# Two layers of linear attention and MLP in split fp32: split weights kept in DRAM, and a set of reorderings

## The chip, the cores and the metric

The kernel runs on one core of one Trainium2 chip. The time is the device time of one execution in microseconds (us), lower is better. A core has a matrix engine (PE, with a queue of its own for weight loads, PEld), a vector engine (DVE), an activation engine (ACT), a third engine for elementwise work (POOL), and SP, which here only issues transfers. Each engine runs its instructions in order. SBUF is the on-chip memory, PSUM the eight banks that PE writes, DRAM the memory outside.

## The reference

Two layers, each an attention block (A) and an MLP block (B) with residuals, on 2048 rows of 576 features, with the same weights in both layers:

```python
def _A_ref(x, wqkv, w_phi, wo):
    q, k, v = ...                                  # 32 heads of 18 features, from x @ wqkv
    pq = jnp.einsum("bhsd,hdf->bhsf", q, w_phi)
    pk = jnp.einsum("bhsd,hdf->bhsf", k, w_phi)
    phi_q = jnp.concatenate([_softmax(pq, axis=-1), _softmax(-pq, axis=-1)], axis=-1)
    phi_k = jnp.concatenate([_softmax(pk, axis=-1), _softmax(-pk, axis=-1)], axis=-1)
    kv = jnp.einsum("bhsf,bhsd->bhfd", phi_k, v)
    z  = jnp.einsum("bhsf->bhf", phi_k)
    num = jnp.einsum("bhqf,bhfd->bhqd", phi_q, kv)
    den = jnp.einsum("bhqf,bhf->bhq", phi_q, z)[..., None] + 1e-6
    return (num / den) @ wo                        # heads joined again

def _B_ref(x, w1, b1, w2, b2):                     # 576 -> 4608 -> 576
    h = relu(x @ w1 + b1) ** 2
    return h @ w2 + b2

for _ in range(2):
    x = x + _A_ref(_layernorm(x), A_wqkv, A_w_phi, A_wo)
    x = x + _B_ref(_layernorm(x), B_w1, B_b1, B_w2, B_b2)
```

kv and z are sums over all 2048 rows: no output of a layer's attention can be made before every row's keys and values are in them.

## The kernel before

*Precision.* Each fp32 matrix is split in a high part (`h`, rounded to the matrix engine's fp32r by a copy on ACT) and a low part (`l`, the rest, by a subtraction on DVE or POOL), and a product of two matrices is three: high x high, low x high, high x low. `piece_tiles` gives the two tiles of one half (288 columns) of a 576x576 weight, 128 partitions x 1440; `wpiece` loads the raw weights into a staging tile (tag "wraw", two buffers) and makes the split; `wpair` does both halves, for v, keys, queries ("q", "k", with w_phi folded in, from the DRAM tensor `wf`) or the output ("o"). The pieces have the tags "whi" and "wlo", two buffers each, so one pair fills them; a few pairs use "s2" and "h1" (TAGS_B) instead.

*Stages.* The rows are four blocks of 512, each of four tiles of 128.
1. `g_fold` multiplies the query and key weights with w_phi, stores them as `wf`, and leaves the split of keys and v in SBUF (`kpair`, `vpair`). The norm of block 0 (`g_norm`) is woven in.
2. Keys and values of the blocks of layer 0 (`g_keys`): `make_v`, `make_raw` (projections, `project`, L435), the softmaxes on DVE, ACT and POOL, then `kv_tile` (L527), which adds one tile's phi_k^T v to the sums.
3. `barrier`: the last keys and the queries of two blocks while the sums are completed, then `sums_operands`, which makes the operands of the next products from the sums (kt, L585, from kq, L580, is its last group of heads), `g_phi`, and `g_out`, the attention's output and norm.
4. `g_mlp` of two blocks (`first`: weights; `hidden`, L820; `square`, L827 to L830; `second`, L838 and L847), each with the attention of other blocks woven in (`back_first`, `back_second`).
5. `g_pair`: the MLP of the last two blocks at once, its first product by the seven-product scheme (`products`, L1128), then its second product for one block with the first and for the other alone (`seconds`, L1147 and L1157). In layer 0 the norms, keys and values of layer 1 for three blocks are woven into `seconds` (`back_keys`).
6. Layer 1 from stage 3.

*Order.* A program lays out each engine's instructions ahead of the run, by their order in the source and by when it expects their inputs. `weave(main, other, rate)` interleaves two generators by the costs that they yield; `tc.issue_after(x)` puts instructions behind instruction x on x's engine; `held(gen, keys)` does so for a whole generator, with x the latest `dense["last"]` (the end of the last `square` on DVE), `dense["squared"]` (its end on ACT) and so on. All transfers of weights, x and hidden values are issued by SP in one order, and a transfer whose buffer is not free holds up those behind it. Work banks of PSUM come from `wtile`: two of tag "w" and the banks in `spare["tags"]`.

The softmax of one tile of keys in stage 2 or 5 ends with POOL's scaling (L495), and `kv_tile` waits for it. In layer 1, `kv_tile` writes a work bank for the first eight tiles, and DVE adds it:

```python
        first = 0 if layer == 0 else (NB - 2) * NT
        if n == first:
            st["ps"] = ps_a.tile([P, TB], F32, tag="acc0", name=f"kvp{layer}")
        ...
        stay, last = n >= first, n == NB * NT - 1
        pt = st["ps"] if stay else wtile(f"{name}k")
```

## Time and profile before

| | |
|---|---|
| median of 3 runs | 2557.3 us (2551.11 to 2559.26) |
| the profiled execution | 2557.62 us, of which 2555.9 us from the first to the last instruction |
| busy, of 2555.9 us | PE 2489.1, DVE 1634.6, ACT 1304.2, POOL 971.8 |
| mean granted clock of PE | 0.991 |
| moved by DMA | 312.99 MB, mean 122 GB/s |
| stages | keys of layer 0 from about 36 us, barriers from 160 and 1410 us, `seconds` of layer 0 from about 1168 to 1388 us |

A row of the waits reads: waiting engine, line and tile, then who released it, total us, times, longest. A row of the timeline reads: start us, length us, engine, line, operation, out<-in, shapes, count, and in brackets the idle time before it with its releaser. A stretch's row gives, for each engine, busy us and number of instructions, then the granted clock of PE, the share of the time that the 16 DMA engines were busy and what they moved.

### The profile page before, as it was taken

How to read it: one execution, taken by the hardware profiler on the slowest of the kernel's cores; microseconds unless marked ns; L12 is line 12 of the kernel's file. 1: busy time of each engine (PE TensorE's matmuls, PEld its weight loads, DVE VectorE, ACT ScalarE, POOL GpSimd, SP SyncE). 2: the span in 40 equal slices, each digit the busy share in tenths (PEclk: the TensorE clock that was granted, in tenths of full speed). 3: DMA queues.
4: the chain of work that ended last, by engine and by line, in shares of the span. 5: the costliest groups of instructions: out<-in, count | busy, mean ns of one | idle time of the engine just before them, and what ended most of it. 6: DMA issues, size and time to landing. Idle time of an engine off the chain costs nothing. (4 is left out here: it accounts for less than half of the span.)

```text
span 2555.9 us, 41504 instructions
## 1 busy us (share of the span) xinstructions
PE 2489.1 (97%) x15108; PEld 2182.6 (85%) x15108; DVE 1634.6 (64%) x2570; ACT 1304.2 (51%) x2293; POOL 971.8 (38%) x1101
## 2 busy tenths in 40 slices
PE   8998999999999999999999989999999999999999
PEld 7998888889888888888889988888888888888888
DVE  7777857555866655555777769484658665555444
ACT  4333555354546666664443435553545466666643
POOL 3544313212335555551434533032123445555322
PEclk9999999999999999999999999999999999999999
DMA  8102432344334433338543133333453344333363
GB/s 252 57 23 72 153 111 83 107 141 165 112 117 126 136 118 98 112 102 265 180 128 115 46 111 110 101 89 107 139 183 90 124 130 144 109 101 104 110 201 128
DMA packets 257224, 312.99 MB, mean 122 GB/s; under 512 B 29818, under 2 KB 175482, under 8 KB 254458
## 3 DMA queue, kind: packets, MB, share of 16 engines
q1 hardware_dynamic: 255760, 307.64, 38.7%
q8 instruction: 118, 1.93, 0.3%
q10 hardware_dynamic: 1258, 2.70, 0.3%
q14 instruction: 88, 0.72, 0.1%
HBM read 255.42 MB, written 54.82 MB: 121 GB/s over the span
## 5 line engine op out<-in xcount | busy, mean ns | idle before, releaser
L1118 POOL TENSOR_TENSOR m_ps<-m_pr,m_ps 128x128 fp32r<-128x128 f32 x144 | 121.9, 847 | 319.2 <-ACT m_ps L1116 264.8
L1117 DVE TENSOR_TENSOR m_ps<-m_pr,m_ps 128x448 fp32r<-128x448 f32 x144 | 93.9, 652 | 153.5 <-ACT m_ps L1116 151.2
L1157 PE MATMUL m_pacc<-m_ps,m_phb 128*128 128x448 f32 x864 | 188.5, 366 | 0.0
L1157 PEld LDWEIGHTS m_pacc<-m_ps,m_phb 128*128 128x128 f32 x864 | 162.2, 188 | 18.0
L1116 ACT ACTIVATE m_ps<-m_pr 128x576 fp32r<-128x576 f32 x144 | 97.9, 680 | 132.3 <-issue 88.5
L1157 PE MATMUL m_pacacc<-m_ps,m_phc 128*128 128x448 f32 x648 | 146.0, 369 | 0.0
L1157 PEld LDWEIGHTS m_pacacc<-m_ps,m_phc 128*128 128x128 f32 x648 | 123.3, 191 | 10.1
L1138 DVE TENSOR_TENSOR m_phb<-m_pz,m_phb 128x512 fp32r<-128x512 f32 x72 | 56.5, 784 | 115.9 <-ACT m_pz L1137 114.4
L820 PE MATMUL m_1ph<-t1onh,m_1h 128*128 128x512 f32 (+1 forms) x380 | 100.7, 390 | 4.5 <-ACT m_1hr L827 2.4
L820 PE MATMUL m_3ph<-t0onh,m_3h 128*128 128x512 f32 (+1 forms) x380 | 98.8, 386 | 2.8 <-ACT m_3hr L827 2.4
L847 PE MATMUL m_2acc<-m_2s,m_2hb 128*128 128x448 f32 x432 | 100.1, 365 | 0.0
L847 PE MATMUL m_0acc<-m_0s,m_0hb 128*128 128x448 f32 x432 | 100.1, 365 | 0.0
L847 PE MATMUL m_3acc<-m_3s,m_3hb 128*128 128x448 f32 x432 | 99.7, 366 | 0.0
L847 PE MATMUL m_1acc<-m_1s,m_1hb 128*128 128x448 f32 x432 | 99.7, 366 | 0.0
L820 PE MATMUL m_0ph<-a_0nh,m_0h 128*128 128x512 f32 (+1 forms) x380 | 97.7, 384 | 0.0
L820 PE MATMUL m_2ph<-a_2nh,m_2h 128*128 128x512 f32 (+1 forms) x380 | 97.7, 384 | 0.0
L847 PEld LDWEIGHTS m_2acc<-m_2s,m_2hb 128*128 128x128 f32 x432 | 81.0, 188 | 10.6 <-ACT m_2hb L828 0.2
L847 PEld LDWEIGHTS m_0acc<-m_0s,m_0hb 128*128 128x128 f32 x432 | 81.0, 188 | 10.7 <-ACT m_0hb L828 0.2
L847 PEld LDWEIGHTS m_3acc<-m_3s,m_3hb 128*128 128x128 f32 x432 | 81.0, 188 | 10.6 <-ACT m_3hb L828 0.2
L847 PEld LDWEIGHTS m_1acc<-m_1s,m_1hb 128*128 128x128 f32 x432 | 81.0, 188 | 10.5
L820 PEld LDWEIGHTS m_1ph<-t1onh,m_1h 128*128 128x128 f32 x380 | 70.2, 193 | 19.2 <-ACT m_1hr L827 3.2
L810 POOL TENSOR_TENSOR m_1s<-m_1r,m_1s 128x128 fp32r<-128x128 f32 x36 | 27.0, 749 | 151.7 <-ACT m_1s L806 134.8
(2504 smaller groups left out, 7464.3 us busy)
## 6 DMA issues: line engine op xcount, KB each, us to landing
m_pr<-in_B_w SPq DMA_DIRECT2D x144, 288.0 KB
m_pr<-in_B_w SPq DMA_DIRECT2D x72, 256.0 KB
hd<-m_pu SPq DMA_DIRECT2D x72, 256.0 KB
m_pg<-hd SPq DMA_DIRECT2D x72, 256.0 KB
m_3r<-in_B_w SPq DMA_DIRECT2D x36, 288.0 KB
m_2r<-in_B_w SPq DMA_DIRECT2D x36, 288.0 KB
m_1r<-in_B_w SPq DMA_DIRECT2D x36, 288.0 KB
m_0r<-in_B_w SPq DMA_DIRECT2D x36, 288.0 KB
```

The costliest lines, as they stand in the source:

```text
L810: nc.gpsimd.tensor_sub(s2[:, D + R : 2 * D], r2[:, R:], s2[:, R:D].bitcast(F32))
L820: nc.tensor.matmul(ph[:, cols], a, m, start=(k == 0), stop=(k == len(ops) - 1))
L847: nc.tensor.matmul(acc[t][:, :R], a[:, rows], m, start=(f == 0 and k == 0), stop=(f == NF - 1 and k == 2))
L1116: nc.scalar.activation(s2[:, :D], r2, AF.Copy)
L1117: nc.vector.tensor_sub(s2[:, D : D + R], r2[:, :R], s2[:, :R].bitcast(F32))
L1118: nc.gpsimd.tensor_sub(s2[:, D + R : 2 * D], r2[:, R:], s2[:, R:D].bitcast(F32))
L1138: nc.vector.tensor_sub(hl, r, hh.bitcast(F32))
L1157: nc.tensor.matmul(accs[b][t][:, :R], a[:, rows], m, start=(g == 0 and k == 0), stop=(g == NF - 1 and k == 2))
```

## The change

1. Split weights in DRAM. `wsplit` holds the high and low parts of v, keys, queries and output. The first two are stored from `vpair` and `kpair` after the fold (`keep_split`); the other two are made in ten steps woven into layer 0's keys (`g_split`). `wpair` then loads the parts into the pieces' tiles, with no staging tile and no split, but for pairs in TAGS_B (the barrier's queries and the last keys of layer 1), which are loaded and split as before.
2. In `g_fold` the norm of block 0 starts three steps later and DVE's part of it is issued behind the latest copy of a fold.
3. `kv_tile` of layer 1 accumulates in the bank acc4 throughout; a block's last tile is issued after the next block's norm, and `spare["tags"]` stays empty in `seconds`.
4. `sums_operands` leaves its last group to a function that `barrier` calls after the other block's queries, its matmuls behind the last projection.
5. `g_features` is held behind "last" and "squared"; the low part of the second weights in the first two steps of an MLP goes behind the norm's last split ("normed").
6. `g_norm` with `fine` takes all four tiles' scaling before the transposes, which become one pipeline; its tile has five buffers.
7. At the end of `g_mlp` the first product of the pair (`then`) comes before the last row sums, and the adds of the last 128 columns come last. At the last product two steps of `back_keys` are taken early.

```diff
+    wsplit = {w: [dram.tile([P, 2 * NC * HP], F32, name=f"ws{w}{p}") for p in "hl"] for w in "qkvo"}
+    def idle(n, gen):
+        yield from (1.0 for _ in range(n))
+        yield from gen
...
-            nc.vector.tensor_copy(wt[:w, : n * P], pt[:w, : n * P])
+            dense["folded"] = nc.vector.tensor_copy(wt[:w, : n * P], pt[:w, : n * P])
...
-    def wpair(which, name, tags=TAGS_A, low=None):
-        if which == "v":
-            return [wpiece(wqkv, 2 * D + h * HP, f"{name}v{h}", tags) for h in range(2)]
+    def wpair(which, name, tags=TAGS_A):
+        if tags is TAGS_B:
+            return [wpiece(wf, (which == "k") * D + h * HP, f"{name}{which}{h}", tags) for h in range(2)]
+        return [wloaded(which, h, f"{name}{which}{h}", tags) for h in range(2)]
+
+    def wloaded(which, half, name, tags):
+        pair = piece_tiles(name, tags)
+        regions = [(slice(0, P), 0, NC)]
         if which == "o":
-            return [wpiece(wo, h * HP, f"{name}o{h}", tags, heads=True, low=low) for h in range(2)]
-        return [wpiece(wf, (which == "k") * D + h * HP, f"{name}{which}{h}", tags) for h in range(2)]
+            regions = [(slice(0, GW), 0, NG - 1), (slice(0, gw[-1]), NG - 1, NG)]
+        for piece, kept in zip(pair, wsplit[which]):
+            for p, c0, c1 in regions:
+                at = half * NC * HP
+                nc.sync.dma_start(piece[p, c0:c1].rearrange("p c n -> p (c n)").bitcast(F32),
+                                  kept[p, at + c0 * HP : at + c1 * HP])
+        return pair
+
+    def keep_split(which, pair):
+        for half in range(2):
+            for piece, kept in zip(pair[half], wsplit[which]):
+                nc.sync.dma_start(kept[:, half * NC * HP : (half + 1) * NC * HP],
+                                  piece.rearrange("p c n -> p (c n)").bitcast(F32))
+
+    def g_split():
+        for c in range(NC):
+            for which in "oq":
+                raw = sb.tile([P, D], F32, tag="r2", name=f"ws{which}r{c}")
+                ...                                   # one load of raw from wo or wf
+                both = cst.tile([P, 2 * NG * GW], F32R, tag="kbh" if which == "o" else "kbl", name=f"ws{which}s{c}")
+                hi, lo = both[:w, :D], both[:w, D : 2 * D]
+                nc.scalar.activation(hi, raw[:w], AF.Copy)
+                yield
+                nc.gpsimd.tensor_sub(lo, raw[:w], hi.bitcast(F32))
+                for part, kept in zip((hi, lo), wsplit[which]):
+                    nc.sync.dma_start(kept[:w].rearrange("p (h c n) -> p h c n", h=2, c=NC)[:, :, c],
+                                      part.rearrange("p (h n) -> p h n", h=2).bitcast(F32))
+                yield
...
-        for half in range(2):
-            for t in range(2):
-                apart(half * 2 + t)
-                yield 2.2
-            yield from pipeline(3, (lambda i: cross(half * 3 + i), lambda i: split(half * 3 + i)), (0.3, 0.6))
+        for t in range(NT):
+            apart(t)
+            yield 2.2
+        yield from pipeline(3 * NT // 2, (cross, split), (0.3, 0.6))
...
-        if n == first:
-            st["ps"] = ps_a.tile([P, TB], F32, tag="acc0", name=f"kvp{layer}")
+        if n == 0:
+            st["ps"] = ps_a.tile([P, TB], F32, tag=f"acc{KC * layer}", name=f"kvp{layer}")
...
-        else:
-            nc.vector.tensor_add(kv, po, kv)
...
+        def last_group():
+            ...                                       # kq as before
+            with tc.issue_after(dense["projected"].ins):
+                for s in range(2):
+                    nc.tensor.matmul(p3[:, s], own[:, s].rearrange("p q f -> p (q f)"),
+                                     place.rearrange("p q d -> p (q d)"), start=True, stop=True)
+            keep(p3, [k[:w, :, last, :w] for k in (kbh, kbl)])
+        return last_group
...
-                                 (2.6, 0.4, 3.0, 2.8, 1.2)))
+                                 (2.6, 0.4, 3.0, 2.8, 1.2)), ("last", "squared"))
...
-        def pieces():
-            with tc.issue_after(behind.ins) if behind else nullcontext():
-                return wpair("o", name, low=nc.gpsimd if parts > 1 else None)
+        pair = wpair("o", name)
...
+            with tc.issue_after(dense["normed"].ins) if behind else nullcontext():
                 nc.vector.tensor_sub(s2[:, D : D + R], r2[:, :R], s2[:, :R].bitcast(F32))
...
+        if then:
+            then()
+        for t in range(NT):
+            ...                                       # the four x tiles are loaded here
         by_rows(NF - 1, range(2), range(3))
...
-        if then:
-            then()
         by_rows(NF - 1, range(2, NT), range(3))
         for t, x in enumerate(after):
             nc.vector.tensor_add(x[:, :R], acc[t][:, :R], x[:, :R])
+        for t, x in enumerate(after):
+            nc.vector.tensor_add(x[:, R:], p3[:, t], x[:, R:])
...
-        sums_operands(layer)
+        last_group = sums_operands(layer)
...
         drain(queries)
+        last_group()
...
-    weave(g_fold(kpair, vpair), g_norm(load_x(0), xT[0], "n0_0"), 0.5)
+    weave(g_fold(kpair, vpair), idle(3, held(g_norm(load_x(0), xT[0], "n0_0"), ("folded",))), 0.5)
+    keep_split("v", vpair)
+    keep_split("k", kpair)
+    splits = g_split()
...                                                   # g_keys: next(splits, None) twice a tile
-                stages = (raw, start, lambda t: soft_exp(es[t]), end, lambda t: None)
-                if not last:
-                    stages += (lambda t: kv_tile(1, vts[t], es[t], f"kv{m}_{t}"),)
+                def keep_sums(t):
+                    if not last:
+                        late.append((vts[t], es[t], f"kv{m}_{t}"))
+                        if len(late) > 1:
+                            kv_tile(1, *late.pop(0))
...
-        drain(products)
-        spare["tags"] = ["acc4"]
-        weave(seconds, iter(()) if layer else back_keys(), 4.0)
+        back = iter(()) if layer else back_keys()
+        for k, _ in enumerate(products):
+            if k == NP - 1:
+                next(back, None)
+                next(back, None)
+        weave(seconds, back, 4.0)
```

## The prediction

> **What bounds the kernel now.** I read the page first, then the waits of the matrix engine (PE), then stretches around its longest waits, and last the queue that issues the loads.

> ```profile
> span 2555.9 us, 41504 instructions
> PE 2489.1 (97%) x15108; PEld 2182.6 (85%) x15108; DVE 1634.6 (64%) x2570; ACT 1304.2 (51%) x2293; POOL 971.8 (38%) x1101
> ...
> PEclk9999999999999999999999999999999999999999
> ```

> PE is busy for 2489.1 of 2555.9 us, so all that an edit can win is in the other 66.8 us and in matmuls that ran slowly. The change neither adds nor drops a matmul that counts (one zeroing matmul moves). DVE at 64% and ACT at 51% have room on average: taking work from them is worth only what PE waits for. That list is the waits of PE (who waited for whom, us in total, times, longest):

> ```profile
> PE kt L585 <- DVE kq L580: 7.4, 2, 4.4
> PE kv_3k L527 <- POOL k_3K3e L495: 6.1, 1, 6.1
> PE kv_3k L527 <- POOL k_2K3e L495: 5.0, 1, 5.0
> PE t0onp L355 <- DVE t0onn L344: 3.8, 4, 1.6
> PE fo L259 <- DVE ft L250: 3.8, 3, 3.1
> PE t1onp L355 <- DVE t1onn L344: 3.1, 4, 1.7
> PE m_ppx L1128 <- DVE m_pu L1241: 2.8, 2, 1.4
> PE m_1ph L820 <- ACT m_1hr L827: 2.4, 1, 2.4
> PE m_3ph L820 <- ACT m_3hr L827: 2.4, 1, 2.4
> PE n_3p L355 <- DVE n_3n L344: 2.3, 1, 2.3
> PE a_1qp L435 <- ACT a_1qs L453: 1.5, 1, 1.5
> PE a_2qp L435 <- ACT a_2qs L453: 1.5, 1, 1.5
> ```

> No wait is long and each is met once or twice; the kernel loses in hand-overs, not in a stage. Behind the longer ones stands a second price. These are stretches right after six waits (length, busy time of PE, its weight loads, DVE, ACT, POOL, then granted clock, DMA share, GB/s):

> ```profile
> 206.60:209.62 3.02, 3.02 (x14) 3.02 (x15) 3.02 (x8) 0.29 (x1) 0.00 (x0) 0.50 0.71 226
> 431.46:434.90 3.44, 3.44 (x8) 2.76 (x9) 2.48 (x4) 2.30 (x4) 0.90 (x1) 0.50 0.18 54
> 1250.76:1254.10 3.34, 3.34 (x70) 3.05 (x71) 2.63 (x5) 0.00 (x0) 1.61 (x2) 0.50 0.45 129
> 1326.79:1332.61 5.82, 5.82 (x77) 5.27 (x78) 2.62 (x5) 0.00 (x0) 1.61 (x2) 0.50 0.61 172
> 1469.30:1472.55 3.25, 3.25 (x15) 3.25 (x16) 3.25 (x9) 0.70 (x2) 0.00 (x0) 0.50 0.00 0
> 1697.75:1701.25 3.50, 3.50 (x8) 2.75 (x9) 2.54 (x4) 2.29 (x4) 0.90 (x1) 0.51 0.21 63
> ```

> PE is never idle in them, but its clock is half. Half of 3.02, 3.44, 3.34, 5.82, 3.25 and 3.50 us is 11.2 us lost beside the waits; a wait of 2.4 us costs about 4.1. [...]

> **The change part by part.** The sum is made against the profiled execution (span 2555.9, its own time 2557.6), which stands 0.3 us from the median of 2557.3, so no correction is needed. Minus is a gain.

> *Key sums of layer 1.* Before, each tile's products go to a work bank and DVE adds them; the last tile of blocks 3 and 2 has PE wait for POOL's scaling (6.1 and 5.0). After, they accumulate in acc4 and that last tile is issued behind the next block's norm. PE meets the product late enough that POOL has long finished, and the removed DVE adds help. 11.1 of waits and 1.7 + 2.9 of clock are at stake; what is late next is the norm of the following block. I take −14 (ends 0 and −15.7).

> *The last group of the sums' operands.* In the barrier PE waits for kq (4.4 and 3.1 us), which DVE reaches late:

> ```profile
> 199.93 4.45 DVE L563 TENSOR_TENSOR kbl<-ko,kbh 126x504 fp32r<-126x504 f32 x2 [0.43 <-ACT kbh L562]
> 204.30 2.25 DVE L580 TENSOR_TENSOR kq<-kv,quarter 128x144 f32<-128x144 f32 x1
> ...
> 199.13 2.91 POOL L309 TENSOR_TENSOR t0oo1l<-t0oo1r,t0oo1h 126x1152 fp32r<-126x1152 f32 x1 [0.25 <-ACT t0oo1h L308]
> ```

> After, those two matmuls and their inputs stand behind the queries' projections, which need nothing from them, and POOL's split of the output weights, running beside DVE's slow pair, is gone: it is a load now. DVE's chain to the scaled queries gets shorter by some of that 4.45 and by the 2.25, so the next wait, for the last scaled tile, should not grow by what PE gains. Waits 7.4, clock 1.5 + 1.6: −9 (ends 0, if the scaled queries are late instead, and −10.5).

> *ACT behind "squared".* The two waits of 2.4 for a relu that queued behind an exponential: the exponential now queues behind the squares. 4.8 + 3.5 of clock, cover is the rest of the softmax, which has a stage of slack: −8 (ends 0, −8.3).

> *First stage.* DVE sits in front of a fold's copy until x has landed:

> ```profile
> 9.80 0.82 DVE L329 BATCH_NORM_STATS2 n_0s<-x 128x6 f32<-128x288 f32 x2 [3.82 <-DMA x<-in_A_x]
> 10.54 0.67 DVE L250 COPY ft<-fp 126x512 f32<-126x512 f32 x1
> ```

> Three idle steps and the order "behind folded" put the norm after the copy. 3.8 of waits; but the norm ends later and the first keys need it: −3 (ends +3, the same chain paid at the other end, and −5.5 with half of a 3.41 us stretch of slow clock).

> *Norm in the barrier's tail, MLP entry.* Waits of 3.8 and 3.1 on DVE. The second-weight remainder moves behind the norm's last split:

> ```profile
> 247.25 1.63 DVE L809 TENSOR_TENSOR m_3s<-m_3r,m_3s 128x448 fp32r<-128x448 f32 x1
> ```

> One such row stands in the norm's chain per layer; the rest of the chain stays: −2.5 (ends 0, −6.9).

> *MLP tail and the pair's first product, early start of the next norm, query evictions.* The row sums queue after the first product and cover DVE's read (2.8): −2.5. Two norm steps are taken before the last product ends (2.3): −2. The evictions of two query tiles wait in ACT behind the output weights' split, which is gone (1.5 twice): −2. Ends of each: 0 and the whole.

> *Writing the splits.* g_split adds ten units (five chunks of rows, for o and for q): one load, an ACT copy and a POOL subtraction of 128x576, two stores; keep_split adds eight stores. By the nearest rows, on ACT and POOL of the same size, and the stages that they run in:

> ```profile
> L1116 ACT ACTIVATE m_ps<-m_pr 128x576 fp32r<-128x576 f32 x144 | 97.9, 680 | 132.3 <-issue 88.5
> ...
> 172.28 1.69 POOL L475 TENSOR_TENSOR k_3K3e<-k_3K3m,k_3ks 128x576 f32<-128x576 f32 x1
> ...
> 36.00:192.00 156.00, 153.44 (x2091) 150.14 (x2091) 120.71 (x177) 58.27 (x116) 73.01 (x58) 1.00 0.23 78
> 32.00:64.00 32.00, 31.77 (x307) 31.39 (x306) 23.04 (x50) 12.27 (x30) 10.93 (x14) 1.00 0.72 243
> ```

> That is 7 us on an ACT busy for 58 of 156 and 17 us on a POOL busy for 73: hidden behind PE's projections. The stores are the risk: v and k, hi and lo, two halves, each 128x1440 of four bytes (737 KB), are 5.9 MB, 24 us at the 243 GB/s of that stretch, on SP's queue ahead of block 1's and 2's x loads. PE has one block of keys (31 us) before it needs them, and tiles of sums lag by two. +1 (ends 0; +10 if DVE stands behind a late x for longer than that lag).

> *Loading the splits.* Twenty weight pairs lose their splits: ACT 1.4 and DVE 1.7 a half, off PE's path but for what is counted above. Each pair now brings 2.95 MB in place of 1.47. Outside one stage it is hidden: between two uses of the buffers lie the softmax or whole MLP steps. That stage is layer 0's second half of the paired MLP with layer 1's keys woven in:

> ```profile
> 1160.00:1390.00 230.00, 216.44 (x1737) 199.99 (x1736) 165.45 (x235) 97.91 (x160) 82.78 (x79) 0.97 0.54 173
> 1190.00:1200.00 10.00, 10.00 (x72) 9.77 (x71) 1.57 (x3) 2.85 (x6) 0.90 (x1) 1.00 1.01 372
> 1200.00:1210.00 10.00, 10.00 (x75) 9.94 (x75) 4.83 (x8) 5.06 (x8) 0.79 (x2) 1.00 0.79 269
> ...
> 1177.30 0.38 SPq L303 DMA_DIRECT2D w_3k0r<-wf  x1
> ...
> 1203.06 1.41 ACT L308 ACTIVATE w_3k0h<-w_3k0r 128x1440 fp32r<-128x1440 f32 x1 [0.79 <-PE v_3pv L435]
> 1204.50 1.66 DVE L309 TENSOR_TENSOR w_3k0l<-w_3k0r,w_3k0h 128x1440 fp32r<-128x1440 f32 x1 [7.75 <-ACT w_3k0h L308]
> 1205.35 0.83 PE L435 MATMUL k_3kp<-w_3k0h,n_3h 128*128 128x288 f32 x5
> ...
> 1282.45 0.77 PE L1157 MATMUL m_pach<-m_ps,m_phc 128*128 128x448 f32 x3
> 1285.56 0.69 PE L435 MATMUL k_2kp<-w_2k0h,n_2h 128*128 128x288 f32 x4
> ```

> This speaks against the change. Today the keys' raw weights are issued at 1177 into a staging buffer, and once v's pieces are free (1203) ACT and DVE fill the buffer in 3.1 us; PE goes on at 1205 without a gap. After, there is no staging: the transfer itself starts when v's pieces are free, 2.95 MB at 269 to 372 GB/s, 8 to 11 us, 2 of which v's last tile covers. PE fills the rest only with second products of the MLP, 3.1 us each (1282.45 to 1285.56), whose own 557 KB come through the same queue. Blocks 3 and 2 have this hand-over. I take two fillers of the three that are needed, so 2.5 us and half a clock stretch of 1.7 each: +8 (ends 0, all filled, and +22, none filled: 2 x (9 + 2)). v of block 3 also comes with twice the bytes just as that stretch fills: +1 (0 to +5). [...]

> *Buffers.* acc4 now holds the sums, so norm and projections in that stage turn over two work banks, not three. A projection lasts 1.8 us and its eviction 0.4; ACT's queue has slack of one, not two: +2 (0 to +6). *Query weights after output weights* in the woven attention come late by one transfer, under MLP steps: +1 (0 to +4).

> Sum: −14 −9 −8 −3 −2.5 −2.5 −2 −2 = −43; +1 +8 +1 +2 +1 = +13; together −30, so 2557.6 − 30 = 2527.

> **The rivals.** *All loads are hidden:* the order of PE is laid out with enough second products at each hand-over; the DMA share of 0.54 over the stage speaks for it. Then +13 shrinks to 1: about 2515. *The loads are exposed:* both hand-overs unfilled and block 3's v late (22 + 5 for 9): 2545. For it: 372 GB/s at share 1.01 at 1190. *Stalls move instead of going:* the chain to the scaled queries, DVE's norm and the late key sums are met again at the next wait; half of 43 stays: 2549. Against it: each wait has independent matmuls right behind it. *Slower, by the hand-over of every pair in that stage:* if all five pairs (three keys, two values) wait for their buffers with no filler, each costs its 8 to 11 us, 2 for the cooled clock, 12 with x loads queued on SP behind the waiting load: 60 in place of 9, 2557.6 − 43 + 4 + 60 = 2579. It decides from about 10 us a pair. Against it: k of block 1 and v have 20 us between uses of the buffers. *The change does not do what it says* (the added orders fall where the order was so already): the waits above show that they do not, so only with the third.

> **How the numbers follow.** Forecast 0.45, 2527, its own range 2518 to 2538; all hidden 0.18; exposed 0.16; moved 0.12; slower 0.09. A measurement of this kernel tells about 0.3%, 7.7 us (its three runs span 2551 to 2559): faster is below 2549.6. Forecast and all hidden with 0.13 of exposed and 0.05 of moved: 0.81; the rest of both, 0.03 and 0.07: 0.10; slower 0.09. Range 2505 to 2558: the low end is all gains whole with the loads hidden, the high end leaves out the slower rival and a little beyond.

> **What would show it.** Right: kt, kv_3k and hr gone from PE's waits; no split of v, k, q, o weights by ACT or DVE except at the first fold, the barrier's q and the last keys; DMA bytes up by some 30 MB of loads and 14 of keeping; the clock at half in fewer stretches. Wrong: PE waiting for a load of k's or v's kept pieces between 1160 and 1390 (hand-overs longer than 5 us), PE waiting at the start for x of block 1, or a longer wait for the scaled queries in the barrier.

## The result, and the profile after

The changed kernel takes 2542.2 us (median of 4 runs, 2541.1 to 2542.9) against 2556.5 (2551.1 to 2559.3): a ratio of 0.9945, 95% interval 0.9929 to 0.9961. It is 14 us faster where 30 were forecast. Its profiled execution took 2541.9 us, a span of 2540.2. From its page:

```profile
span 2540.2 us, 41516 instructions
...
PE 2482.4 (98%) x15108; PEld 2178.7 (86%) x15108; DVE 1587.9 (63%) x2518; ACT 1263.9 (50%) x2251; POOL 960.1 (38%) x1103
...
DMA packets 254451, 352.65 MB, mean 139 GB/s; under 512 B 30502, under 2 KB 161318, under 8 KB 251686
...
q8 instruction: 118, 1.93, 0.3%
```

PE is idle for 57.8 us in place of 66.8, and DMA moves 352.65 MB in place of 312.99; the last row, the queue that carries instructions, is needed further down. PE's waits, in the same columns as before:

```profile
PE n_2p L405 <- DVE n_2l L400: 9.8, 2, 9.6
PE kvp L560 <- issue: 4.9, 1, 4.9
PE t1onp L391 <- DVE t1onn L380: 4.4, 4, 2.0
PE n_0p L391 <- DVE n_0n L380: 4.4, 4, 2.6
PE t0onp L391 <- DVE t0onn L380: 3.6, 4, 1.6
PE n_2p L391 <- DVE n_2n L380: 2.4, 2, 1.8
PE t0q3qp L471 <- DVE t0q0l L304: 1.9, 1, 1.9
...
PE a_1qp L471 <- ACT a_1qs L489: 1.6, 1, 1.6
PE a_2qp L471 <- ACT a_2qs L489: 1.6, 1, 1.6
...
PE k_3kp L471 <- DMA w_3k0h<-wskh: 1.0, 1, 1.0
```

The waits that were to go are gone: kt, both kv_3k, both hr. One wait for a kept part is left, of 1.0 us. But five waits are new or longer: 9.6 us at block 2's norm in layer 1, 4.9 us in the key sums of the barrier, 2.6 at block 0's norm at the start, 1.8 at block 2's norm in layer 0, 1.9 at the barrier's queries. Behind or around the longer ones PE runs at half clock (length, busy times, then granted clock, DMA share, GB/s):

```profile
29.21:39.45 10.24, 8.04 (x36) 7.41 (x37) 9.02 (x19) 3.34 (x8) 4.12 (x5) 0.50 0.91 285
175.99:179.40 3.41, 3.41 (x16) 3.41 (x16) 3.41 (x6) 0.00 (x0) 0.70 (x1) 0.50 0.02 5
203.29:210.12 6.83, 4.82 (x23) 4.74 (x24) 1.35 (x1) 2.05 (x3) 0.00 (x0) 0.50 0.38 127
1254.60:1264.84 10.24, 3.67 (x11) 3.21 (x12) 6.88 (x14) 0.38 (x1) 2.33 (x4) 0.50 0.77 253
```

Laying the first and last matmul of each product in the two traces side by side shows where time moved. Up to the end of the barrier's v in layer 0 the changed kernel had *lost* 10.1 us (3.8 at the first projection, 3.7 more in block 1's keys, the rest at the barrier's queries), then 3 more at the 4.9 us wait; the barrier gave 5.4 back, the hold behind the squares 4.6, the MLP's end and the early norm about 6. It entered layer 1's keys 3.5 us ahead, lost 6 at the wait of 9.6, won 7 at the next block, 5 in layer 1's barrier and 5 at its squares.

### The profile page after: what moved, and what is told of

It reads as the page before. It is cut to its first block, busy times and chain, and to the rows that moved or that the text cites. A ratio compares the mean times of both kernels' runs of the same rounds, so it can differ in the third digit from the quotient of the medians.

```text
span 2540.2 us, 41516 instructions
## 1 busy us (share of the span) xinstructions
PE 2482.4 (98%) x15108; PEld 2178.7 (86%) x15108; DVE 1587.9 (63%) x2518; ACT 1263.9 (50%) x2251; POOL 960.1 (38%) x1103
## 2 busy tenths in 40 slices
DMA packets 254451, 352.65 MB, mean 139 GB/s; under 512 B 30502, under 2 KB 161318, under 8 KB 251686
## 4 chain that ended last, share of the span: by engine, by line
PE 69%; DVE 3%; ACT 2%; DMA 2%; POOL 1%; issue 1%; SPq 1%; DVEq 0%; POOLq 0%; ACTq 0%
PE m_ppx L1159 8%; PE m_pacc L1188 6%; PE m_1ph L850 5%; PE m_0ph L850 4%; PE m_pacacc L1188 4%; PE m_2ph L850 4%; PE m_ppy L1159 4%; PE m_0acc L877 3%; PE m_1acc L877 3%; PE m_2acc L877 3%; PE m_ppz L1159 2%; PE m_pacc L1178 2%; PE m_pacacc L1178 2%; PE m_pach L1188 1%; PE a_0po L785 1%; PE m_0acc L868 1%
## 5 line engine op out<-in xcount | busy, mean ns | idle before, releaser
L1147 ACT ACTIVATE m_ps<-m_pr 128x576 fp32r<-128x576 f32 x144 | 97.9, 680 | 123.3 <-issue 61.1
L877 PEld LDWEIGHTS m_2acc<-m_2s,m_2hb 128*128 128x128 f32 x432 | 80.9, 188 | 10.5 <-ACT m_2hb L858 0.2
L877 PEld LDWEIGHTS m_0acc<-m_0s,m_0hb 128*128 128x128 f32 x432 | 80.9, 188 | 10.5 <-ACT m_0hb L858 0.2
```

What stands on the lines that cost most here:

```text
L877: nc.tensor.matmul(acc[t][:, :R], a[:, rows], m, start=(f == 0 and k == 0), stop=(f == NF - 1 and k == 2))
L1147: nc.scalar.activation(s2[:, :D], r2, AF.Copy)
```

## The experiments

Two losses had to be explained, the shift in layer 0 and the wait of 9.6 us. Theory A put both down to the kept splits (stores and loads on SP's queue and the DMA engines). The rivals: the ten steps that make the splits stand in the way on ACT and POOL; and the new order of the norm, or the missing work bank, makes the wait. Each kernel ran beside the kernel before on the same chip, whose medians were 2554.1 to 2557.6; a difference of under some 3 us between two rows of this table says little.

| kernel | median us (range) | ratio to before, 95% |
|---|---|---|
| changed | 2542.2 (2541.1 to 2542.9) | 0.9945, 0.9929 to 0.9961 |
| x1_raw: item 1 undone | 2536.4 (2533.3 to 2537.9) | 0.9920, 0.9908 to 0.9933 |
| x2_only: item 1 alone | 2554.7 (2546.7 to 2559.1) | 0.9988, 0.9977 to 0.9998 |
| x3_fold: item 2 undone | 2541.9 (2539.9 to 2543.4) | 0.9943, 0.9931 to 0.9955 |
| x4_late: v's and keys' stores later | 2545.6 (2542.7 to 2549.6) | 0.9955, 0.9942 to 0.9968 |
| x5_norm: item 6 undone | 2532.0 (2530.7 to 2533.7) | 0.9902, 0.9889 to 0.9916 |
| x6_sums: key sums of item 3 undone | 2551.2 (2548.9 to 2555.5) | 0.9975, 0.9964 to 0.9987 |
| x7_lazy: splits at first use | 2531.2 (2530.4 to 2533.0) | 0.9899, 0.9886 to 0.9913 |
| x8_gate: barrier's loads later | 2536.6 (2534.4 to 2537.1) | 0.9918, 0.9906 to 0.9931 |
| x9_both: x5 and x7 | 2518.6 (2516.7 to 2520.2) | 0.9855, 0.9842 to 0.9869 |
| x10_spread: x9, products spread | 2522.6 (2521.3 to 2523.8) | 0.9872, 0.9857 to 0.9887 |
| x11_both_fold: x9, item 2 undone | 2519.0 (2518.3 to 2519.6) | 0.9857, 0.9843 to 0.9870 |
| x12_group: item 4 undone | 2542.8 (2539.6 to 2544.6) | 0.9949, 0.9936 to 0.9961 |
| x13_raw_norm: items 1 and 6 undone | 2536.1 (2529.9 to 2537.3) | 0.9924, 0.9912 to 0.9936 |
| x14_squared: hold behind the squares undone | 2549.5 (2545.8 to 2554.7) | 0.9978, 0.9966 to 0.9989 |
| x15_best: x9, spread in layer 0 only | 2518.5 (2517.2 to 2522.7) | 0.9857, 0.9843 to 0.9872 |
| x16_both_sums: x9, key sums undone | 2531.8 (2527.2 to 2533.3) | 0.9903, 0.9889 to 0.9916 |

**Item 1 away, and item 1 alone.** The edits are the kernel before's `wpiece`, `wpair` and `pieces` put into the changed kernel, and the reverse.

> The changed kernel with its first item undone: every pair is loaded raw and split on chip again, nothing is kept in DRAM. Theory A (the kept splits cost PE time): the shift of about 9 us that the changed kernel collects between block 1's keys and the start of the barrier in layer 0 (longest waits 1.83, 1.92 and 4.87 us) goes, and so does the wait of 9.56 us of PE at 1261 for the low part of block 2's norm, because x no longer stands on SP's queue behind twice the weight bytes: 2542 - 9 - 8 = about 2525, less 3 us or so that the output weights' split takes back in the barriers: 2525 to 2530. Rival B (the order of the norms, the banks and the fold's order cause these losses, the kept splits are free): the 9.56 us wait stays, the time is 2540 to 2548.

> The kernel before with the first item alone: splits kept in DRAM and loaded, all orders as before. Theory A: slower, by the 9 us of layer 0's keys and by up to 8 in the second products with the keys of layer 1, less up to 3 won in the barriers: 2557 + 6 to 14 = 2563 to 2571. Rival B: the loads are hidden as the stores are, and the splits taken from ACT and DVE help the barriers: 2550 to 2558. The waits of 7.4 (kt), 6.1 and 5.0 (kv_3k) and 2.4 us (hr) stay in both.

Without item 1 the changed kernel is 6 us faster, between the theories, and its wait at block 2's norm falls from 9.6 to 5.8 us: it neither goes nor stays. Item 1 alone makes the kernel before 2 us faster, as rival B had it, in runs that scatter over 12 us. So its parts work against each other, and the trace of item 1 alone shows a loss plainly. Rows of POOL, DVE and PE around block 1's first tiles:

```profile
71.36 1.44 POOL L342 TENSOR_TENSOR wsos<-wsor,wsos 126x576 fp32r<-126x576 f32 x1
73.67 0.55 DVE L373 TENSOR_SCALAR n_2n<-x,n_2m,n_2d 128x512 f32<-128x512 f32 x1 [3.33 <-POOL n_2d L361]
...
81.80 0.55 DVE L513 RECIPROCAL K_3r<-K_3r 128x64 f32<-128x64 f32 x1
82.49 1.43 POOL L342 TENSOR_TENSOR wsos<-wsor,wsos 126x576 fp32r<-126x576 f32 x1 [3.65 <-ACT wsos L340]
83.87 2.15 POOL L524 TENSOR_TENSOR K_3e<-K_3e,K_3r 128x1152 f32<-128x1152 f32 x1
...
88.50 0.35 DVE L374 TENSOR_SCALAR n_2e<-x,n_2m,n_2d 128x128 f32<-128x128 f32 x1 [2.77 <-POOL n_2d L361]
...
94.23 0.93 PE L464 MATMUL k_1p<-w0k0h,n_1h 128*128 128x288 f32 x5 [3.48 <-ACT vslot L473]
```

A split step (wsos) stands ahead of the keys' scaling on POOL. The scaling of K_3 starts at 83.87; in the kernel before it starts at 77.60, with the same PE time up to there:

```profile
77.60 2.15 POOL L495 TENSOR_TENSOR K_3e<-K_3e,K_3r 128x1152 f32<-128x1152 f32 x1 [3.65 <-DVE K_3r L484]
```

Of these 6.3 us, the step at 82.49 itself costs 1.5, since DVE's factor K_3r was ready at 82.35. The other 4.8 came before: DVE was late by then, and had waited 3.33 us for POOL's n_2d, which stood behind the scaling of K_2 and the split step at 71.36. From there POOL, DVE (which waits for n_2d again) and ACT are all late, and PE waits 3.48 us. In the changed kernel ACT stands before its evictions: 3.68 us for a load, with half of k_1s behind it.

```profile
101.33 0.41 ACT L489 ACTIVATE k_1s<-k_1p 128x288 f32<-128x288 f32 x1
105.42 0.69 ACT L344 ACTIVATE wsqs<-wsqr 128x576 fp32r<-128x576 f32 x1 [3.68 <-DMA wsqr<-wf]
106.02 0.39 ACT L489 ACTIVATE k_1s<-k_1p 128x288 f32<-128x288 f32 x1
```

The steps also act through SP. Their stores wait there for ACT's and POOL's halves (3.4 and 2.2 us), and the second part of that load and the next x come behind them. DVE waits 2.87 us for this x, ahead of its work on the same keys:

```profile
98.07 0.85 SPq L348 DMA_DIRECT2D wsoh<-wsos  x1
101.22 0.80 SPq L348 DMA_DIRECT2D wsol<-wsos  x1
102.07 0.53 SPq L210 DMA_DIRECT2D wsqr<-wf  x1
102.70 1.00 SPq L1314 DMA_DIRECT2D x<-in_A_x  x2
...
106.03 0.82 DVE L362 BATCH_NORM_STATS2 n_3s<-x 128x6 f32<-128x288 f32 x2 [2.87 <-DMA x<-in_A_x]
```

**The start, and the stores.**

```diff
-    weave(g_fold(...), idle(3, held(g_norm(...), ("folded",))), 0.5)     # x3_fold
+    weave(g_fold(...), g_norm(...), 0.5)
...
-    keep_split("v", vpair)                                               # x4_late: k after block 1,
-    keep_split("k", kpair)                                               # v after block 2
```

> The changed kernel with its second item undone: block 0's norm starts with the fold and is not held behind the fold's copies. Theory A (the held norm makes block 0's keys late): first value projection back from 39.7 to about 36 us, and with the slow clock of 29 to 39 us back at 11.6 to 15: 2542 - 5 = 2536 to 2539. Rival B (the keys are late because of v's and k's pieces or of the stores): first projection still at about 39 us, 2541 to 2543.

> The changed kernel with the eight stores of keep_split put later: those of the keys after block 1's keys, those of v after block 2's. Theory A (5.9 MB of stores on SP ahead of the x loads of block 1 make DVE late): the two shifts of 2.0 and 1.9 us at 101 and 111 us go, 2538 to 2539. Rival B (the ten steps that make the splits of output and queries do it, on ACT, POOL and in their stores): the shift at 111 us stays, 2541 to 2544.

With item 2 undone the first projection comes at 36.5 in place of 39.7, as theory A had it, and yet the time is the same: block 1 then waits 3.3 and 1.5 us for ACT's evictions, and the gain is gone by the end of that block. Moving the stores did not help either (rival B): block 1 then waits 4.7 us for ACT. What holds the keys up is not the 5.9 MB of stores of v and keys but the split steps, with their own loads and stores.

**The splits at first use.** No steps beside layer 0's keys; the first pair "o" and the first pair "q" are loaded raw and split, and `keep_split` stores them as it does v and keys.

```diff
-    splits = g_split()
+        if which not in kept_yet:
+            kept_yet.add(which)
+            pair = [wpiece(...) for h in range(2)]
+            keep_split(which, pair)
+            return pair
         return [wloaded(which, h, f"{name}{which}{h}", tags) for h in range(2)]
```

> The changed kernel without the ten steps that split the output and query weights beside layer 0's keys: their first use in layer 0 loads them raw and splits them as before, and the parts are stored from there; every later use loads them. Theory S (those steps stand on ACT and POOL ahead of the evictions and the scaling of the keys and wait there for their loads): block 1's shift of 3.9 us goes, the wait for the barrier's split falls from 1.92 to 0.9, and, since the barrier loads half the bytes, the pause of 4.87 us in the last key sums falls to about 2: 2542 - 4 - 2.5 - 3 = 2531 to 2534. Rival (the eight stores of v and k are the cause): block 1's shift stays, 2538 to 2541.

As theory S had it: 11 us faster. Block 1's waits are gone, the barrier's queries wait 0.9 us, the pause in the key sums is 2.0 us.

**The pause in the key sums.**

```diff
+            sent = nc.sync.dma_start(kvs[layer], sums[layer]["kv"]...)
+            with tc.issue_after(sent.ins):
+                pair = wpair("o", name)
```

> The changed kernel with the output weights' loads of both barriers put behind a small store of the finished key sums on SP's queue (the store is added, 147 KB): the same bytes, some 8 us later. Theory I (PE pauses in the third of three key-sum products in a row for its instructions, and for longer while the 16 DMA engines are busy: 1.85 and 2.04 us at a DMA share of 0.01, 4.87 to 6.42 us at 0.9): the pause at 200.4 falls from 4.87 to about 2 and the one of 0.71 at 1460.7 goes: 2542 - 4.5 = 2537 to 2539, if the weights still come before their use at 230.8. Rival (the pause has another cause): it stays at 4.9, 2541 to 2543.

The same bytes, later: the pause is 2.2 us and the time 5.6 us shorter. PE's rows before and after the pause, in the changed kernel and in the kernel before:

```profile
199.69 0.75 PE L560 MATMUL kvp<-k_3K3e,vslot 128*32 128x36 f32 x62
205.30 0.33 PE L560 MATMUL kvp<-k_3K3e,vslot 128*32 128x36 f32 x2 [4.87 <-issue]
```

```profile
189.59 0.75 PE L527 MATMUL kvp<-k_3K3e,vslot 128*32 128x36 f32 x62
192.19 0.23 PE L527 MATMUL kvp<-k_3K3e,vslot 128*32 128x36 f32 x2 [1.85 <-issue]
```

The DMA queues for half a microsecond from 202.5 in the changed kernel, and from 189.5 in the kernel before (packets, MB, share of the 16 engines):

```profile
q1 hardware_dynamic: 32, 0.15, 83.4%
q8 instruction: 1, 0.02, 14.1%
```

```profile
q8 instruction: 1, 0.02, 11.7%
```

In each case one packet of instructions passes, and PE goes on 2.7 to 2.9 us after the start of that half microsecond (189.5 to 192.2; 202.5 to 205.3; with the loads put later, 199.5 to 202.4). Counted from the start of the third product (199.69, and 189.59 before) the packet comes some 3 us later in the changed kernel, among the weights' packets that fill 83.4% of the engines.

**The wait of 9.6 us.**

```diff
-        for t in range(NT):                                              # x5_norm: item 6 undone
-            apart(t)
-            yield 2.2
-        yield from pipeline(3 * NT // 2, (cross, split), (0.3, 0.6))
+        for half in range(2):
+            for t in range(2):
+                apart(half * 2 + t)
+                yield 2.2
+            yield from pipeline(3, ...)
...
-            st["ps"] = ps_a.tile([P, TB], F32, tag=f"acc{KC * layer}", ...)   # x6_sums: as before,
+        pt = st["ps"] if stay else wtile(f"{name}k")                      # acc4 a work bank again
```

> The changed kernel with its sixth item undone: the norm of layer 1's blocks goes in halves again, two tiles' scaling and then their transposes, with two buffers for the scaled tile. Theory N (the wait of 9.56 us at 1261 is DVE's: the moments of block 0's first tiles stand ahead of block 2's splits, because all scaling comes first, and wait 3.94 us for x): the wait falls to under 3 us and the 0.50 clock of 1254 to 1265 goes with it, some 10 us, while the 4.5 us won at the first transposes of block 3's norm are lost: 2534 to 2539. Rival P (two work banks are the cause, since they hold PE at the transposes whatever the order on DVE): a wait of over 6 us stays there and the time is 2541 to 2548.

> The changed kernel with the key sums of its third item undone: products into a work bank, added by DVE, acc4 back as a third work bank. Theory P (two banks): the 9.56 us wait goes, but PE waits for the scaled last tile of blocks 3 and 2 again (6.1 and 5.0 us before, 3.7 and 3.2 with the splits loaded): 2542 - 13 + 10 = 2536 to 2542. Theory N (order on DVE): the wait of 9.56 us becomes a wait of 3 us or more at the following use of the third bank and the two waits come back beside it: 2545 to 2552. That the key sums are worth 14 us, as forecast, would show as 2552 or more.

Theory N holds: with the norm in halves the wait is 1.1 us and the time 10 us shorter. The rows of DVE, SP and PE in the changed kernel:

```profile
1250.69 0.95 DVE L1233 TENSOR_TENSOR m_phc<-m_pg,m_phc 128x512 fp32r<-128x512 f32 x1
1255.59 0.82 DVE L362 BATCH_NORM_STATS2 n_0s<-x 128x6 f32<-128x288 f32 x2 [3.94 <-DMA x<-xs]
...
1259.05 0.82 DVE L362 BATCH_NORM_STATS2 n_0s<-x 128x6 f32<-128x288 f32 x2 [0.21 <-DMA x<-xs]
...
1260.43 1.29 DVE L400 TENSOR_TENSOR n_2l<-n_2p,n_2h 128x512 fp32r<-128x512 f32 x2
...
1246.91 0.38 SPq L320 DMA_DIRECT2D w_2v1l<-wsvl  x1
1250.32 0.33 SPq L1145 DMA_DIRECT2D m_pr<-in_B_w  x1
...
1251.17 0.90 SPq L1437 DMA_DIRECT2D x<-xs  x2
...
1261.17 0.69 PE L405 MATMUL n_2p<-ident,n_2e 128*128 128x128 f32 x2 [9.56 <-DVE n_2l L400]
```

ACT's half of block 2's split was done at 1251. DVE's (n_2l) stood behind the moments of block 0, the block after, whose x SP issued at 1251.17. Ahead of it on SP stood a kept part of v's weights (1246.91) and second weights of the MLP (m_pr): for their buffers SP had waited 8.8 us for DVE, up to 1245.9, and 2.8 for POOL, up to 1250.3. With only two work banks PE could do nothing meanwhile. In halves, n_2l comes first. With the third bank back and the key sums as before (x6_sums) that wait goes too, but the key sums wait 7.7 and 6.9 us for POOL, longer than before.

**Together, and what each gain belongs to.**

> The changed kernel with both repairs: the norm of layer 1's blocks in halves again, and the output and query weights split at their first use and stored from there. Theory (two separate losses, one at the waits of layer 0's keys and barrier, one at the wait of 9.56 us): they add, 2542 - 11 - 10 = 2521, within 2518 to 2524. Rival (both free the same slack, or the halves of the norm suffer from the loads that come closer): 2526 to 2531.

> The kernel with both repairs and the second item undone: block 0's norm starts with the fold and is not held. Theory C (the second item only moves the start's waits: 3.4 us at the fold's copy against 2.56 and four of some 0.7 at the first transposes): first value projection between 36 and 37 us in both, time within 1.5 us of the kernel with both repairs. Rival D (the second item is worth the 3 us of the forecast once the split steps are gone): 2.5 to 4 us slower than the kernel with both repairs.

The two repairs add: 2518.6 us. PE's longest waits are then of the kind that the kernel before had in its barriers and at its start:

```profile
PE t1onp L390 <- DVE t1onn L379: 4.4, 4, 2.0
PE n_0p L390 <- DVE n_0n L379: 3.7, 3, 2.6
PE t0onp L390 <- DVE t0onn L379: 3.6, 4, 1.7
PE kvp L560 <- issue: 2.1, 1, 2.1
```

Item 2 is worth nothing there (0.4 us, inside the scatter): theory C. The key-sum products spread, by a projection's halves before the last two:

```diff
+                else:
+                    half_raw(xprev, 0, qpair, t + 2 - NT, raws2[0], f"{n}q{prev}q")
                 kv_tile(layer, vts[t], kes[t], f"{n}{t}")
```

> The kernel with both repairs, and in the barriers the halves of one tile's query projection of the other block are put before each of the last two key-sum products, so that no three of these products (64 small matmuls each) follow one another; no matmul is added. Theory I (PE runs out of instructions after some 190 small matmuls in a row): the pause of 2.04 us in layer 0 goes, with the slow clock behind it 3 to 4 us: 2517 to 2519. Rival (the pause moves to the next products, or the sums come late for the barrier's chain): as the kernel with both repairs, or up to 3 us slower.

> The kernel with both repairs, and one query tile's halves put between the last key-sum products in layer 0's barrier alone. Theory I (what that spread won in layer 0, 2.4 us at the start of the first MLP, stays won; the 3.4 us that it lost were in layer 1's barrier, where no pause is): 2515 to 2517. Rival (the gain was one of start-up, not of the pause): 2518 to 2520.

The pause is gone from both traces, but spread in both layers it costs 4 us between medians: layer 1's barrier had no pause, and its chain got later by 3.4. In layer 0 alone the time is that of the kernel with both repairs, though the profiled span was 2.4 us shorter: its first projection came at 34.8 in place of 36.4, in a stage where the two do not differ, so the start's scatter covers 1.6 of it, and a gain is not shown.

> The changed kernel with its fourth item undone: the last group of the sums' operands stands before the other block's queries again. Theory (its two waits of 4.4 and 3.1 us and the slow clock behind them are what it won): 2542 + 10.5 = 2552, within 2549 to 2554, with both waits in the list again. Rival (the loaded output weights had taken POOL's split away, and with it most of the wait): the waits come back at under half their length, 2543 to 2547.

> The changed kernel with the hold of the queries' softmax behind the squares undone (the second half of the fifth item). Theory (the two waits of 2.4 us for a relu and the slow clock behind each are won by this hold): 2542 + 8 = 2549 to 2552, with two waits of about 2.4 us back in m_3ph and m_1ph. Rival (as with the last group, another item had taken the wait away): 2541 to 2544, no such waits.

The last group undone changes nothing (2542.8), and its wait is 0.8 us, not the 7.4 of before (rival). The hold undone costs 7 us, and its waits are back whole. From the two lists:

```profile
PE kt L614 <- DVE kq L609: 0.8, 2, 0.5
```

```profile
PE m_1ph L850 <- ACT m_1hr L857: 2.4, 1, 2.4
PE m_3ph L850 <- ACT m_3hr L857: 2.4, 1, 2.4
```

> The changed kernel with the first and the sixth item undone: weights loaded raw and split on chip, the norm of layer 1's blocks in halves. Beside the kernel with both repairs it differs in the kept splits alone. Theory V (keeping pays once its splits are made at first use, by what DVE, ACT and POOL no longer do in layer 1's barrier, 4.3 us, and in its MLPs, 3 us): 2536 - 9 = 2525 to 2529, 7 to 10 us slower than the kernel with both repairs (2518.6). Rival (kept splits are worth nothing): 2517 to 2521.

> The kernel with both repairs and the third item undone: key sums of layer 1 into work banks, added by DVE. Theory (the forecast's term is right where nothing else stands in its way): the two waits for the scaled last tiles are back at 6 to 7 us each and the slow clock with them: 2518.6 + 14 = 2531 to 2536. Rival (the waits are shorter once the norm goes in halves): 2522 to 2527.

With both repairs, keeping the splits is worth 17 us between medians, more than the 7 to 10 expected, and 9.7 between the profiled executions (2529.9 and 2520.2). In these two traces the raw kernel is 1.8 us ahead after the start, 4.8 behind at the end of layer 1's keys, where PE waits 4.7 us for n_2l and not 1.1, and 5.0 more behind after layer 1's barrier. The raw kernel's other runs, at 2535 to 2537, were not profiled, so what the rest is stays open.

The key sums are worth 13 us. Their two waits are shorter than expected, 3.2 and 3.1; the last add of layer 1's barrier makes PE wait 1.8 more, PE runs at clock 0.50 for 10.2 us after the second and the third of these waits, which costs half of that (the mean granted clock of the profiled executions is 0.993, with both repairs 0.995), and some 2 us are the start's scatter.

```profile
PE kv_3k L563 <- POOL k_3K3e L531: 3.2, 1, 3.2
PE kv_3k L563 <- POOL k_2K3e L531: 3.1, 1, 3.1
```

## Why the prediction was right in sign and twice too large

The gains summed to 43 and the costs to 13. Most of the gains came; two costs were several times too small.

- **Writing the splits, +1: measured +11** (x7_lazy). This step failed first. It added 7 us on ACT and 17 on POOL to engines that were busy for 58 and 73 of 156 us, and called them hidden. The sum of their work was hidden; their place was not. On ACT a step that waited 3.68 us for its load held half of an eviction behind it (105.42 above), and on POOL one that had waited 3.65 us for ACT stood ahead of K_3's scaling (82.49, x2_only). The risk named was the stores ahead of x on SP. For the eight stores of v and keys x4_late and x7_lazy show it harmless; the steps' own stores did put DVE behind a late x, by 2.87 us. Laid beside x7_lazy, the changed kernel's trace loses 2.4 us at the start, 4.0 in block 1's keys, 2.5 at the barrier's queries and 3.6 at the pause in the key sums, which no term had.
- **The norm's new order: no term, about +10** (x5_norm). The nearest were the buffers, +2 (0 to +6), and the working of the key sums, which did say that the next block's norm is late next, at no price. The order put the moments of a later block ahead of the split that PE was waiting for, and their x stood on SP behind the weights. It costs this beside the loaded parts alone: with raw weights undoing it changes nothing between medians (x1_raw 2536.4, x13_raw_norm 2536.1), and PE waits there for n_2l either way, 5.8 and 4.7 us. Why the old order waits nearly as long there stays open.
- **Loading at the hand-overs, +8: about +1**, a wait of 1.0 at block 3 and none at block 2. Second products filled the gaps, as in the rival of hidden loads.
- **Key sums, −14:** the term was right in size, 13 us where nothing stands in the way (x16_both_sums) and 9 in the changed kernel (x6_sums). In the changed kernel's trace hardly anything of it is left, because the wait of 9.6 comes in the same place.
- **The last group, −9:** right, 10.5 us by the traces. But it belongs to either of two edits: with raw weights the reordering leaves a wait of 0.8 at kt (x1_raw), and loading the output weights' parts, without the reordering, leaves 0.8 (x12_group) or 1.4 (x2_only). The second of them adds nothing.
- **ACT behind the squares, −8:** right, 7 us by x14_squared and 4.6 in each layer by the traces.
- **First stage, −3:** failed. The changed kernel's first projection of values came 3.8 us later; undone, the gain at the start was lost again behind ACT. It takes the split steps as well: without them, and with the item in place, that projection came at 36.7 (x7_lazy), 0.8 later than before, and with the repairs the item makes no difference.
- **Norm in the tail, −2.5:** about −1, in layer 1 alone. **MLP's end, −2.5:** about that. **Early norm, −2:** −4.5. **Query evictions, −2:** nothing, 1.6 us each and 1.5 before: they queued behind something other than the splits.

With these sizes the sum is −13 − 10.5 − 8 − 1 − 2.5 − 4.5 = −39.5 and +11 + 10 + 1 = +22, together −17.5, against the −14.3 measured.

Two counts were off, with no term resting on them: 18 pairs lose their splits, not twenty, and DMA moved 39.7 MB more, not 44.

The time, 2542, lies between the forecast's own range (to 2538) and the rival of moved stalls (2549). By mechanism it was that rival in two places: a wait that took the place of the one removed, on DVE in layer 1's keys and on POOL and ACT in layer 0's.

Half clock behind waits was met as forecast, and behind shorter ones too: the wait of 1.92 us that ended at 174.66 was followed by it (175.99 above). Length alone does not decide: after the wait of 2.31 us that ended at 1186.33 in the kernel before the clock stayed at 1.00 (mean from 1186.33 to 1190.00). What decides it no run shows.

## What to carry to other kernels

Work moved to an engine with room was hidden here only where nothing urgent stood behind it in that engine's order while it waited for its own input (3.68 us on an ACT that is busy for 50% of the span); look at what it waits for, not at the engine's share. A split, or any other preparation that is to be kept, was best made where it was made anyway, at its first use (11 us, x7_lazy). When a wait is removed, follow each engine's queue past that place once more: where edits meet, as the norm's order, the missing bank and the loaded parts did, each alone may look free.
